# Giving one of the last attention block's two normalisation multiplies to ScalarE instead of VectorE

## The chip, the cores and the metric

The kernel runs on one core of one Trainium2 chip. The metric is device time in microseconds (us). The kernel before takes 1286.9 us (median of 6 runs, 1286.76 to 1287.05). Engines are named as the profile names them: PE is the matmul side of TensorE and PEld its weight loads, DVE is VectorE, ACT is ScalarE, POOL is GpSimd, SP is the engine that starts the DMAs.

I use one measure, which I call **the tail**: from the start of the first reciprocal of the last attention block to the end of the last add on VectorE.

## The reference, cut to what matters

```python
xn = layernorm(A_x)                              # 2048 x 512
q  = (xn @ wq) -> 32 heads of 128
p  = softmax(q @ k_cache^T * 128**-0.5)          # 2048 keys per head
o  = p @ v_cache
s  = concat_heads(o) @ wo                        # 2048 x 512
g  = silu(reglu_mlp(xn))                         # gate, up, down; 2048 x 512
return x + s * g
```

## The kernel before

The MLP runs first and leaves `g_sb`. Then 128 blocks follow, one for each head and each 512 queries (`QB` = 4 blocks a head). A block runs 16 score tiles, the exponential on ScalarE, and 16 PV steps which accumulate in two PSUM banks, two groups of 128 queries in each. Column 128 of V holds a constant, so each group's column 128 of the accumulator is the softmax denominator (`z_ap`). The last block is normalised bank by bank, to let the second half of the work start early:

```python
def emit_norm_last(b, bank, pvtok):
    ...
    _wait(dve, pvtok)                            # PV of this bank is complete
    o_ap, z_ap = acc_view()
    js = slice(2 * bank, 2 * bank + 2)
    rtok = sem_rz.sig(dve.reciprocal(rz_sb[:, js, :], z_ap[:, js, :]))
    _wait(dve, rtok)
    tok = sem_norm.sig(
        dve.tensor_tensor(Onorm[ob][:, js, :], o_ap[:, js, :],
                          rz_sb[:, js, :].to_broadcast([128, 2, Dh]), ALU.mult))
    emit_last_transposes(hh, Q, ob, bank, tok)   # queued; PE does them later
    return tok
```

After the last block, eight of the 16 output tiles remain (tiles 8 to 15, 128 rows each). Tiles 8 to 11 don't need the last block; tiles 12 to 15 do, through four transposes on PE and two copies on ScalarE:

```python
for n in range(NT - 8, NT - 4, 2):               # tiles 8,9 then 10,11
    emit_M([(emit_final_tile, n), (emit_final_tile, n + 1)])
    if n == NT - 8:
        flush_last_transposes()                  # PE: between tile 9 and tile 10
for n in range(NT - 4, NT, 2):                   # tiles 12..15
    emit_M([(emit_final_tile, n), (emit_final_tile, n + 1)])
flush_final_add()
```

A final tile is four matmuls on PE, a multiply with `g_sb` on VectorE (from PSUM into `fin_tmp`), and an add to `x_sb` on VectorE. The add of a tile is issued after the multiply of the next one:

```python
def emit_final_tile(n, bank):
    ...                                          # 4 matmuls into ps_r, signal otok
    _wait(dve, otok)
    _wait(dve, fin_free[fb])
    mtok = sem_opa.sig(
        dve.tensor_tensor(fin_tmp[fb][:], ps_r[:, bank, 0:D], g_sb[:, n, :], ALU.mult))
    flush_final_add()                            # x_sb += fin_tmp of the tile before, then its output DMA
    fin_pending.append((n, fb, mtok))
    return mtok
```

The softmax here doesn't subtract the row's maximum and nothing guards it: scores larger than these inputs give would overflow.

## Time and profile before

| what | value | how to read it |
|---|---|---|
| time | 1286.9 us | median of 6 runs |
| span of the profile | 1284.6 us | first to last instruction |
| PE busy | 1278.8 us, 100% | the whole is bound by TensorE |
| VectorE busy in the tail | 8.89 of 8.96 us | busy time by stretch; the tail runs at VectorE's pace |
| last multiply's end to the span's end | 2.8 us | the last add and the last output DMA |

The first lines of the page of the kernel before, and its chain of work that ended last, by engine (the chain is followed back from the last instruction, at each step to what released it; shares are of the span):

```profile
span 1284.6 us, 26946 instructions
...
PE 1278.8 (100%) x12040; PEld 835.2 (65%) x12040; DVE 380.6 (30%) x685; ACT 1001.7 (78%) x1109; POOL 13.2 (1%) x25
...
PE 99%; DVE 1%; ACT 0%; issue 0%; DVEq 0%
```

Over the whole span PE is the limit. The 1% of VectorE in the chain is the tail, which is the only place that the change touches. The next lines are from the timeline of the kernel before. The columns are start, duration (both in us), engine, line, operation, output and inputs, shapes, count of merged instructions, and in square brackets the idle time of the engine before it and what ended that. L779 is the matmuls of a final tile, L787 its multiply, L803 its add, L714 the transposes, L693 and L696 the reciprocal and the multiply of the normalisation.

```profile
1269.85 1.89 PE L779 MATMUL ps_r<-Wo_sb,OT_store 128*128 128x512 bf16 x8
1270.91 0.69 DVE L787 TENSOR_TENSOR fin_tmp<-ps_r,g_sb 128x512 bf16<-128x512 f32 x1 [3.31 <-PE ps_r L779]
...
1273.39 1.89 PE L779 MATMUL ps_r<-Wo_sb,OT_store 128*128 128x512 bf16 x8
1273.48 0.17 DVE L693 RECIPROCAL rz_sb<-ps_acc 128x2 f32<-128x2 f32 x1 [0.61 <-PE ps_acc L742]
1273.68 0.42 DVE L696 TENSOR_TENSOR Onorm<-ps_acc,rz_sb 128x256 bf16<-128x256 f32 x1
1274.02 0.16 DVE L693 RECIPROCAL rz_sb<-ps_acc 128x2 f32<-128x2 f32 x1
1274.22 0.42 DVE L696 TENSOR_TENSOR Onorm<-ps_acc,rz_sb 128x256 bf16<-128x256 f32 x1
1274.56 0.68 DVE L787 TENSOR_TENSOR fin_tmp<-ps_r,g_sb 128x512 bf16<-128x512 f32 x1
1274.90 0.42 PEld L714 LDWEIGHTS ps_r<-ident,Onorm 128*128 128x128 bf16 x4
1275.12 0.39 PE L714 MATMUL ps_r<-ident,Onorm 128*128 128x128 bf16 x4
...
1275.34 5.34 PE L779 MATMUL ps_r<-Wo_sb,OT_store 128*128 128x512 bf16 x24
...
1275.49 0.69 DVE L787 TENSOR_TENSOR fin_tmp<-ps_r,g_sb 128x512 bf16<-128x512 f32 x1
...
1276.42 0.69 DVE L787 TENSOR_TENSOR fin_tmp<-ps_r,g_sb 128x512 bf16<-128x512 f32 x1
...
1281.09 0.69 DVE L787 TENSOR_TENSOR fin_tmp<-ps_r,g_sb 128x512 bf16<-128x512 f32 x1
1281.69 0.75 DVE L803 TENSOR_TENSOR x_sb<-x_sb,fin_tmp 128x512 bf16<-128x512 bf16 x2
```

Three readings matter.

- The tail is 8.96 us: from 1273.48 to 1281.69 + 0.75 = 1282.44. Multiplies start every 0.933 us (1274.56 to 1281.09 is seven steps), with an add between two of them and no idle time noted on VectorE. PE delivers a tile every 0.864 us (four matmuls of 0.216 us each: eight take 1.73 us in the chain of work), so VectorE is the slower of the two in the tail, by little.
- Where VectorE did wait for a final tile, its multiply came 1.06 us after the tile's first matmul (1269.85 to 1270.91). Call this the lead.
- PE's first matmul of tile 8 is at 1273.39 and that of tile 10 at 1275.34. With the lead, their multiplies cannot start before 1274.45 and 1276.40. They start at 1274.56 and 1276.42. So PE is only 0.11 and 0.02 us ahead of VectorE there.

### The profile page before, as it was taken

Reading aid. Unit: us, or ns where it says so; the run is one execution under the profiler, and the core shown is the slowest. Engines: PE = TensorE matmul, PEld = TensorE weight load, DVE = VectorE, ACT = ScalarE, POOL = GpSimd, SP = SyncE. Lnnn points to the kernel's source line nnn. Section 1 sums busy time; section 2 is a strip of 40 time slices with the busy share of each in tenths; the row PEclk is TensorE's granted clock in tenths of the full one; section 3 lists DMA queues with packets and bytes.
Section 4 is the critical chain, followed back from the end, with each engine's and each line's share of the span. In section 5 each row is a group of like instructions: output and inputs, shape, how many; then the busy total and the mean of one; then the engine's idle time right before and its main releaser. Section 6 shows DMA issues by size and latency. Waiting matters only on the chain.

```text
span 1284.6 us, 26946 instructions
## 1 busy us (share of the span) xinstructions
PE 1278.8 (100%) x12040; PEld 835.2 (65%) x12040; DVE 380.6 (30%) x685; ACT 1001.7 (78%) x1109; POOL 13.2 (1%) x25
## 2 busy tenths in 40 slices
PE   9999999999999999999999999999999999999998
PEld 5444476666666666666666666666666666666665
DVE  6433311112222222222222222222222222234455
ACT  3322399998888888888888888888888888888884
POOL 2100000000000000000000000000000000000000
PEclk9999999999999999999999999999999999999999
DMA  9600123232222332332321322323323312333202
GB/s 262 131 1 1 22 48 53 62 55 38 36 53 46 71 55 50 55 70 51 54 47 31 66 47 53 55 67 55 55 51 71 54 34 38 51 67 55 51 13 75
DMA packets 240977, 72.13 MB, mean 56 GB/s; under 512 B 227808, under 2 KB 240864, under 8 KB 240864
## 3 DMA queue, kind: packets, MB, share of 16 engines
q1 hardware_dynamic: 240048, 69.76, 28.5%
q8 instruction: 96, 1.57, 0.5%
q10 hardware_dynamic: 816, 0.66, 0.2%
q14 instruction: 17, 0.14, 0.0%
HBM read 32.77 MB, written 2.10 MB: 27 GB/s over the span
## 4 chain that ended last, share of the span: by engine, by line
PE 99%; DVE 1%; ACT 0%; issue 0%; DVEq 0%
PE ps_acc L742 36%; PE ps_r L645 34%; PE ps_r L578 9%; PE ps_r L599 8%; PE ps_acc L511 4%; PE ps_r L488 4%; PE ps_r L492 4%; PE ps_r L779 1%; DVE fin_tmp L787 0%; PE ps_r L402 0%; PE ps_r L374 0%; DVE x_sb L803 0%; ACT gr_sb L454 0%; PE ps_acc L364 0%; ACT xcT L369 0%
## 5 line engine op out<-in xcount | busy, mean ns | idle before, releaser
L655 ACT ACTIVATE PT<-ps_r 128x1024 bf16<-128x1024 f32 x1024 | 952.5, 1054 | 167.7 <-PE ps_r L645 167.7
L742 PEld LDWEIGHTS ps_acc<-V_sb,PT 128*128 128x128 bf16 x8192 | 620.9, 98 | 241.8 <-ACT PT L655 3.5
L742 PE MATMUL ps_acc<-V_sb,PT 128*128 128x129 bf16 x8192 | 776.9, 220 | 0.0
L645 PE MATMUL ps_r<-QT_sb,KT_sb 128*128 128x512 bf16 x2048 | 754.5, 379 | 0.0
L672 DVE RECIPROCAL rz_sb<-ps_acc 128x4 f32<-128x4 f32 x127 | 23.2, 183 | 729.8 <-PE ps_acc L742 729.8
L645 PEld LDWEIGHTS ps_r<-QT_sb,KT_sb 128*128 128x128 bf16 x2048 | 194.9, 98 | 1.1 <-DVE QT_sb L589 0.4
L578 PE MATMUL ps_r<-xnT,Wq_sb 128*128 128x512 bf16 x512 | 130.9, 379 | 0.0
L599 PE MATMUL ps_r<-Wo_sb,OT_store 128*128 128x512 bf16 x448 | 114.6, 379 | 0.0
L589 DVE CAST QT_sb<-ps_r 128x512 bf16<-128x512 f32 x128 | 88.5, 691 | 48.2 <-PE ps_r L578 48.2
L578 PEld LDWEIGHTS ps_r<-xnT,Wq_sb 128*128 128x128 bf16 x512 | 49.8, 97 | 60.7 <-ACT PT L655 27.1
L675 DVE TENSOR_TENSOR Onorm<-ps_acc,rz_sb 128x512 bf16<-128x512 f32 x127 | 87.8, 691 | 4.4
L599 PEld LDWEIGHTS ps_r<-Wo_sb,OT_store 128*128 128x128 bf16 x448 | 43.8, 98 | 52.9 <-ACT PT L655 0.2
L454 ACT ACTIVATE gr_sb<-ps_r 128x512 bf16<-128x512 f32 x56 | 32.9, 595 | 49.2 <-PE ps_r L488 48.7
L612 DVE TENSOR_TENSOR s_acc<-s_acc,ps_r 128x512 f32<-128x512 f32 x96 | 66.0, 687 | 17.4 <-PE ps_r L599 17.4
L460 DVE TENSOR_TENSOR hT<-gr_sb,ps_r 128x512 bf16<-128x512 bf16 x56 | 38.4, 685 | 46.9 <-PE ps_r L492 42.2
L511 PE MATMUL ps_acc<-Wd_sb,hT 128*128 128x512 bf16 x224 | 49.0, 379 | 0.0
L492 PE MATMUL ps_r<-xnT,Wu_sb 128*128 128x512 bf16 x168 | 43.1, 379 | 0.0
L488 PE MATMUL ps_r<-xnT,Wg_sb 128*128 128x512 bf16 x168 | 43.1, 379 | 0.0
L511 PEld LDWEIGHTS ps_acc<-Wd_sb,hT 128*128 128x128 bf16 x224 | 21.9, 98 | 26.5 <-DVE g_sb L528 0.3
L519 ACT ACTIVATE sig_sb<-ps_acc 128x512 f32<-128x512 f32 x12 | 7.2, 597 | 29.5 <-PE ps_acc L511 29.5
L492 PEld LDWEIGHTS ps_r<-xnT,Wu_sb 128*128 128x128 bf16 x168 | 16.4, 98 | 19.8
L488 PEld LDWEIGHTS ps_r<-xnT,Wg_sb 128*128 128x128 bf16 x168 | 16.4, 98 | 19.8
(50 smaller groups left out, 182.1 us busy)
## 6 DMA issues: line engine op xcount, KB each, us to landing
V_sb<-in_A_v_cache_dram SPq DMA_DIRECT2D x32, 512.0 KB, 4.6
Wq_sb<-in_A_wq_dram SPq DMA_DIRECT2D x32, 128.0 KB, 2.5
Wo_sb<-in_A_wo_dram SPq DMA_DIRECT2D x8, 512.0 KB, 4.9
OT_store<-Onorm SPq DMA_TRANSPOSE x127, 2.4
Wd_sb<-in_B_W_down_dram SPq DMA_DIRECT2D x1, 1792.0 KB, 14.6
x_sb<-in_A_x_dram SPq DMA_DIRECT2D x3, 512.0 KB, 12.1
out_dram<-x_sb SPq DMA_DIRECT2D x6, 256.0 KB, 2.2
Wg_sb<-in_B_W_gate_dram SPq DMA_DIRECT2D x1, 768.0 KB, 12.0
```

What stands on the lines that cost most here:

```text
L460: dve.tensor_tensor(hT[par][:, fc, :], gr_sb[gk][:], ps_r[:, gb + 1, :], ALU.mult)
L488: ins = pe.matmul(ps_r[:, gb, :], Wg_sb[:, c, fs], xT[:, c, xs], start=(c == 0), stop=(c == DC - 1))
L492: ins = pe.matmul(ps_r[:, gb + 1, :], Wu_sb[:, c, fs], xT[:, c, xs], start=(c == 0), stop=(c == DC - 1))
L511: ins = pe.matmul(ps_acc[:, jb, 0:D], hT[par][:, fc, j * 128:(j + 1) * 128], Wd_sb[:, fc, :], start=(fc == 0), stop=(fc == FC - 1))
L578: ins = pe.matmul(ps_r[:, bank, :], Wq_sb[b][:, c, :], xnT[:, c, qs], start=(c == 0), stop=(c == DC - 1))
L589: etok = sem_qpe.sig(dve.tensor_copy(QT_sb[b][:, qs], ps_r[:, bank, :]))
L599: ins = pe.matmul(ps_r[:, bank, 0:D], OT_store[g % 2][:, hh, n * 128:(n + 1) * 128], Wo_sb[g % 2][:, hh, :], start=(hh == 0), stop=(hh == ...
L612: dve.tensor_tensor(s_acc[:, n, :], s_acc[:, n, :], ps_r[:, bank, 0:D], ALU.add)
L645: ins = pe.matmul(ps_r[:, 2 * s + tt, :], KT_sb[h % 2][:, t * 128:(t + 1) * 128], QT_sb[h % 2][:, qs], start=True, stop=True)
L655: act.activation(PT[pb][:], ps_r[:, 2 * s:2 * s + 2, :], ACTF.Exp, scale=scale)
L675: dve.tensor_tensor(Onorm[ob][:], o_ap, rz_sb[:].to_broadcast([128, 4, Dh]), ALU.mult))
L742: ins = pe.matmul(o_ap, PT[pb][:, tt, j * 128:(j + 1) * 128], V_sb[vb][:, t, 0:VW], start=(t == 0 and j % 2 == 0), stop=(t == KT - 1 and j ...
```

## The change

The intent: VectorE is busy all through the tail and ScalarE is idle from the last exponential until it copies the transposes. So ScalarE takes the multiply of bank 0, as two activations with function Copy and the reciprocal as a per-row scale. VectorE is to go straight on to bank 1.

```diff
                     rtok = sem_rz.sig(dve.reciprocal(rz_sb[:, js, :], z_ap[:, js, :]))
+                    if bank == 0:
+                        _wait(act, rtok)
+                        for j in range(2):
+                            tok = sem_otc.sig(
+                                act.activation(Onorm[ob][:, j, :], o_ap[:, j, :], ACTF.Copy,
+                                               scale=rz_sb[:, j, 0:1]))
+                        emit_last_transposes(hh, Q, ob, bank, tok)
+                        return tok
                     _wait(dve, rtok)
```

## The prediction

> **What bounds it now.** TensorE. The page's busy shares give PE 1278.8 of 1284.6 us (100%), ACT 78%, DVE 30%; the chain that ended last is 99% PE, 1% DVE. The change touches only the last block's tail, after its last PV matmul (about 1273.5 us), so at most the last 11 us can move. There the chain in order of time leaves PE and runs on VectorE: reciprocal 1273.48, multiply 1273.68, reciprocal 1274.02, multiply 1274.22, then eight final multiply/add pairs (fin_tmp, x_sb) at 1274.56, 1275.49, 1276.42, ..., 1281.09, every 0.933 us, then the last output DMA.
>
> **Removed.** One 128x256 multiply on VectorE, 0.42 us (start to next start 0.34 us in the timeline).
>
> **Added.** Two 128x128 ACTIVATE Copy on ScalarE, idle from 1271.4 to 1275.4 us. The Trainium skill, "ScalarE: Activation LUTs", section "What ACT_TABLE_LOAD costs", gives 186 ns + 0.833 ns per column, 93 ns more per pointer operand, 93 ns overlap: estimate 386 ns each, about 0.68 us for both. The trace agrees on the operand: Tanh 128x512 took 687 ns with a pointer scale, 597 without. No table load: the section "Table sets" says copy is in every set, and the built program shows none. They should run at about 1273.75 to 1274.45.
>
> **Moved.** The second reciprocal follows the first at once (about 1273.65, once the last PV matmul has signalled), its multiply at about 1273.85, done at 1274.27. PE's order is unchanged.
>
> **How much is on the critical path.** VectorE could start final tile 8 at about 1274.2, but must wait for PE. Where VectorE was idle before, the first multiply came 1.06 to 1.07 us after its tile's first matmul (1269.85 to 1270.91; 1264.58 to 1265.65). Tile 8's first matmul starts at 1273.39 and does not move, so its multiply can't start before 1274.45: 0.11 us earlier than now, not 0.34. Tile 9 could follow at 1275.38. Tile 10's matmuls begin at 1275.34, behind the four transposes, which stand behind tile 9's matmuls, not behind the normalisation (first weight load 1274.90; Onorm done at 1274.64). So tile 10's multiply can't start before 1276.40; today it starts at 1276.42. The remaining gain is about 0.02 us, and from there VectorE's 0.933 us cadence is what it was. The transposes need ScalarE's result by 1274.90; estimated ready at 1274.45, so PE should not wait.
>
> **Predicted time:** 1287.0 us (gain 0.0 to 0.1 us, below the 0.3 us spread of the runs); 8 in 10 between 1286.0 and 1288.0. Chances: faster by over 2% 0.005, within 2% 0.985, slower 0.01.
>
> **What would show each step.**
> - Timeline: two Onorm activations on ScalarE of 0.3 to 0.4 us each, both done before 1274.9; no table load.
> - VectorE's two reciprocals adjacent, one 0.42 us multiply, then a new short wait of VectorE for PE before tile 8's multiply, about 0.2 us.
> - Tile 8's multiply 1.06 us after its first matmul; tile 10's at 1276.40 on the old clock; from the last PV matmul to the end of the span unchanged within 0.1 us.
> - Transposes still directly behind tile 9's matmuls, no idle of PE ahead of them.
>
> **What would make it wrong.** A hidden table load (1.28 us each in this trace): ScalarE would end near 1275.7, the transposes and PE would slip about 0.6 us and the tail with them, still only 0.05%. ScalarE and VectorE slowing each other on the accumulator banks. A much later wake-up of ScalarE. None reaches 2%; the total can leave the range only by a state of the chip, not by this edit.

## The result, and the profile after

The changed kernel took 1286.92 us (median of 6 runs, 1286.44 to 1287.22), the kernel before 1286.9 us (6 runs of the same rounds). The ratio is 1.0, with a 95% interval of 0.9987 to 1.0013: the same.

The top of the page of the changed kernel:

```profile
span 1285.3 us, 26720 instructions
...
PE 1267.7 (99%) x11813; PEld 835.9 (65%) x12040; DVE 380.5 (30%) x684; ACT 1002.3 (78%) x1111; POOL 13.3 (1%) x25
```

The counts show the edit: one instruction fewer on VectorE (685 to 684) and two more on ScalarE (1109 to 1111). PE's lower busy time is not a gain. Its matmul records are 11813 against 12040 weight loads, so 227 records are missing from this trace, and the weight loads are complete. (The chain of this page also runs through ScalarE for 12% of the span where the other ran through PE alone; the exponentials are unchanged, so I draw nothing from it.)

The timeline of the changed kernel in the tail. The added lines moved the line numbers: here L787 is the matmuls of a final tile, L795 its multiply, L811 its add, L722 the transposes, L698 the new activations, L704 the one multiply left to VectorE.

```profile
1274.20 0.28 DVE L693 RECIPROCAL rz_sb<-ps_acc 128x2 f32<-128x2 f32 x2 [0.61 <-PE ps_acc L750]
1274.32 1.67 PE L787 MATMUL ps_r<-Wo_sb,OT_store 128*128 128x512 bf16 x7
1274.40 0.63 ACT L698 ACTIVATE Onorm<-ps_acc,rz_sb 128x128 bf16<-128x128 f32 x2 [2.29 <-DVE rz_sb L693]
1274.51 0.42 DVE L704 TENSOR_TENSOR Onorm<-ps_acc,rz_sb 128x256 bf16<-128x256 f32 x1
1275.17 0.69 DVE L795 TENSOR_TENSOR fin_tmp<-ps_r,g_sb 128x512 bf16<-128x512 f32 x1 [0.23 <-PE ps_r L787]
1275.62 0.42 PEld L722 LDWEIGHTS ps_r<-ident,Onorm 128*128 128x128 bf16 x4
...
1275.84 0.39 PE L722 MATMUL ps_r<-ident,Onorm 128*128 128x128 bf16 x4
...
1276.06 5.34 PE L787 MATMUL ps_r<-Wo_sb,OT_store 128*128 128x512 bf16 x24
1276.11 0.68 DVE L795 TENSOR_TENSOR fin_tmp<-ps_r,g_sb 128x512 bf16<-128x512 f32 x1
...
1277.12 0.69 DVE L795 TENSOR_TENSOR fin_tmp<-ps_r,g_sb 128x512 bf16<-128x512 f32 x1
...
1281.80 0.69 DVE L795 TENSOR_TENSOR fin_tmp<-ps_r,g_sb 128x512 bf16<-128x512 f32 x1
1282.40 0.75 DVE L811 TENSOR_TENSOR x_sb<-x_sb,fin_tmp 128x512 bf16<-128x512 bf16 x2
```

Of the eight matmuls of tiles 8 and 9 the first is not in this trace (x7, from 1274.32), so the lead of tile 8 can't be read here. That of tile 10 can: 1276.06 to 1277.12, again 1.06 us.

The tail began 0.72 us later in this execution (1274.20 against 1273.48), which is all of the difference between the two spans and not the change's doing (see kernel 2), so compare each event by its distance from the first reciprocal:

| us after the first reciprocal | before | after |
|---|---|---|
| last multiply of the normalisation on VectorE ends | 1.16 | 0.73 |
| ScalarE's two activations end | – | 0.83 |
| multiply of tile 8 starts | 1.08 | 0.97 |
| the transposes start on PE | 1.64 | 1.64 |
| multiply of tile 9 starts | 2.01 | 1.91 |
| multiply of tile 10 starts | 2.94 | 2.92 |
| multiply of tile 15 starts | 7.61 | 7.60 |
| last add on VectorE ends (the tail) | 8.96 | 8.95 |

VectorE's normalisation ends 0.43 us earlier. That is more than the 0.34 us of the multiply, because the second reciprocal now starts 0.11 us after the first (0.28 - 0.17), where a multiply used to start only 0.20 us after it. Of the 0.43 us, tile 8 gets 0.11 us. A new wait for PE takes 0.24 us (0.97 - 0.73; the profile puts 0.23 in brackets), and the last 0.08 us is an overlap that is lost: before, tile 8's multiply started 0.08 us ahead of the end of the normalisation (1.08 against 1.16). Tile 10 gets 0.02 us, because its matmuls stand behind the transposes, which have not moved. From there on VectorE is at its own pace again and the end moves by 0.01 us.

### The profile page after: what moved, and what is told of

It reads as the page before. It is cut to its first block, busy times and chain, and to the rows that moved or that the text cites. A ratio compares the mean times of both kernels' runs of the same rounds, so it can differ in the third digit from the quotient of the medians.

```text
span 1285.3 us, 26720 instructions
## 1 busy us (share of the span) xinstructions
PE 1267.7 (99%) x11813; PEld 835.9 (65%) x12040; DVE 380.5 (30%) x684; ACT 1002.3 (78%) x1111; POOL 13.3 (1%) x25
## 4 chain that ended last, share of the span: by engine, by line
PE 86%; ACT 12%; issue 1%; DVE 0%; DVEq 0%
PE ps_acc L750 32%; PE ps_r L645 25%; ACT PT L655 12%; PE ps_r L578 9%; PE ps_r L599 8%; PE ps_acc L511 4%; PE ps_r L492 4%; PE ps_r L488 4%; PE ps_r L787 1%; PE ps_r L374 0%; PE ps_r L402 0%; DVE fin_tmp L795 0%; DVE x_sb L811 0%; ACT gr_sb L454 0%; PE ps_acc L364 0%
## 5 line engine op out<-in xcount | busy, mean ns | idle before, releaser
L645 PE MATMUL ps_r<-QT_sb,KT_sb 128*128 128x512 bf16 x1837 | 675.1, 379 | 0.3
```

The source lines that it names most:

```text
L645: ins = pe.matmul(ps_r[:, 2 * s + tt, :], KT_sb[h % 2][:, t * 128:(t + 1) * 128], QT_sb[h % 2][:, qs], start=True, stop=True)
```

## The experiments

**Theory.** VectorE is the slower engine in the tail, but PE follows it so closely that time taken off VectorE ahead of tile 8 is turned into waits for PE, at tile 8 and at tile 10. **Rival.** The 0.34 us that a multiply costs in VectorE's stream is really there to be had, and ScalarE's version eats it: through its two activations, its wake-up, or both engines reading the accumulator. In the experiments "mult" and "add" are VectorE's instructions for a final tile. All nine kernels passed the comparison with the reference. That includes the first one, which leaves out a multiply, so that comparison is too coarse to see it.

### 1. Nobody does bank 0's multiply

```diff
 # against the changed kernel
                     if bank == 0:
-                        _wait(act, rtok)
-                        for j in range(2): ... act.activation(...)
-                        emit_last_transposes(hh, Q, ob, bank, tok)
-                        return tok
+                        emit_last_transposes(hh, Q, ob, bank, rtok)
+                        return rtok
```

> Bank 0's multiply left out altogether (no engine does it; wrong result in 256 rows on purpose). Tail = from the start of the first reciprocal of the last block to the end of the last add on VectorE; before 8.96 us, after 8.95 us. Theory (TensorE sets the pace at tiles 8 and 10, so VectorE time saved ahead of them is not worth anything): tail 8.93 to 8.97, tile 8's multiply 0.97 us after the first reciprocal, tile 10's 2.92 us. Rival (the saved 0.34 us is eaten by ScalarE's version: its two activations, its wake-up, the shared accumulator bank): tail near 8.6.

From the timeline of this kernel: the reciprocals, tile 8's multiply and the last adds.

```profile
1274.01 0.28 DVE L693 RECIPROCAL rz_sb<-ps_acc 128x2 f32<-128x2 f32 x2 [0.61 <-PE ps_acc L745]
...
1274.99 0.69 DVE L790 TENSOR_TENSOR fin_tmp<-ps_r,g_sb 128x512 bf16<-128x512 f32 x1 [0.24 <-PE ps_r L782]
...
1282.21 0.75 DVE L806 TENSOR_TENSOR x_sb<-x_sb,fin_tmp 128x512 bf16<-128x512 bf16 x2
```

The tail was 8.95 us, tile 8's multiply came 0.98 us and tile 10's 2.93 us after the first reciprocal, and VectorE waited 0.24 us for PE at tile 8. One run took 1286.94 us against 1286.84 us for the kernel before. So the multiply for free is worth as much as the multiply on ScalarE: nothing. The rival falls; ScalarE's version costs nothing that a cheaper one would have given back.

### 2. VectorE does bank 0's multiply twice

```diff
 # against the kernel before
                     _wait(dve, rtok)
+                    if bank == 0:
+                        sem_norm.sig(dve.tensor_tensor(scr[:, 0:2, :], o_ap[:, js, :],
+                                     rz_sb[:, js, :].to_broadcast([128, 2, Dh]), ALU.mult))
                     tok = sem_norm.sig(
```

> The kernel before, with VectorE doing bank 0's multiply a second time, into a scratch buffer. Theory (before, VectorE runs back to back through the tail, with TensorE 0.02 to 0.1 us ahead, so the tail is open to added VectorE time though not to saved time): every multiply from tile 8 on is 0.34 us later, tail 9.28 to 9.32. Rival (VectorE has real slack in the tail and the whole of it is TensorE's): tail under 9.05.

From the timeline of this kernel: first reciprocal, tile 8's multiply, and the last adds.

```profile
1274.96 0.17 DVE L694 RECIPROCAL rz_sb<-ps_acc 128x2 f32<-128x2 f32 x1 [0.61 <-PE ps_acc L747]
...
1276.38 0.68 DVE L792 TENSOR_TENSOR fin_tmp<-ps_r,g_sb 128x512 bf16<-128x512 f32 x1
...
1283.51 0.75 DVE L808 TENSOR_TENSOR x_sb<-x_sb,fin_tmp 128x512 bf16<-128x512 bf16 x2
```

Tile 8's multiply is 1.42 us after the reciprocal (1.08 before) and the tail is 9.30 us (8.96 before): the added 0.34 us comes through whole. One multiply more costs 0.34 us, one multiply fewer gives 0.01 us. VectorE's work is on the path, and still there is nothing to gain by shortening it ahead of tile 8. The single run took 1288.23 us, 1.39 us more than the kernel before; only 0.34 us of that is the tail. The tail simply began late in this execution (1274.96). The profiled executions of all kernels here begin it between 1273.43 and 1274.96 us. The traces show where that comes from: the first score matmul starts between 144.0 and 145.5 us, and from there to the first reciprocal of the last block all eleven profiled executions take 1129.4 or 1129.5 us. So the shift arises in the first 144 us, in code that the change doesn't touch. In this execution the first matmul on the gate weights waited 1.37 us for their DMA and started at 7.71 us, against 6.21 us in the kernel before.

### 3 and 4. The transposes between tiles 10 and 11, without and with the change

```diff
 # the same edit, once against the kernel before and once against the changed kernel
-                for n in range(NT - 8, NT - 4, 2):
-                    emit_M([(emit_final_tile, n), (emit_final_tile, n + 1)])
-                    if n == NT - 8:
-                        flush_last_transposes()
+                emit_M([(emit_final_tile, NT - 8), (emit_final_tile, NT - 7)])
+                s = ring_acquire()
+                m0 = emit_final_tile(NT - 6, 2 * s)
+                flush_last_transposes()
+                m1 = emit_final_tile(NT - 5, 2 * s + 1)
+                ring_tok[s] = [m0, m1]
```

> The kernel before, with the four transposes of the last block moved from between final tiles 9 and 10 to between 10 and 11. Theory: VectorE is back to back here, so an earlier tile 10 is of no use: tail 8.95 to 8.97. Rival (before is TensorE-bound at tile 10 as well): tail shorter by up to 0.2, 8.75 to 8.85.

> The changed kernel with the same move of the transposes. Theory: tile 10's matmuls start 0.22 us earlier, so its multiply no longer waits for TensorE and comes at 2.83 us after the first reciprocal; tile 11 becomes the gate at about 3.79 (3.87 before): tail 8.86 to 8.89, so 0.07 to 0.1 of the saved time comes through. Rival (nothing of the saved time is there to be had, or ScalarE's share eats it): tail 8.95.

Without the change the tail was 8.97 us, from the first and the last line here: no gain.

```profile
1273.97 0.17 DVE L693 RECIPROCAL rz_sb<-ps_acc 128x2 f32<-128x2 f32 x1 [0.61 <-PE ps_acc L742]
...
1282.19 0.75 DVE L803 TENSOR_TENSOR x_sb<-x_sb,fin_tmp 128x512 bf16<-128x512 bf16 x2
```

With it, from the timeline:

```profile
1273.87 0.28 DVE L693 RECIPROCAL rz_sb<-ps_acc 128x2 f32<-128x2 f32 x2 [0.61 <-PE ps_acc L750]
...
1276.37 0.39 PE L722 MATMUL ps_r<-ident,Onorm 128*128 128x128 bf16 x4
...
1276.71 0.68 DVE L795 TENSOR_TENSOR fin_tmp<-ps_r,g_sb 128x512 bf16<-128x512 f32 x1
...
1277.65 0.69 DVE L795 TENSOR_TENSOR fin_tmp<-ps_r,g_sb 128x512 bf16<-128x512 f32 x1
...
1282.00 0.75 DVE L811 TENSOR_TENSOR x_sb<-x_sb,fin_tmp 128x512 bf16<-128x512 bf16 x2
```

Tile 10's multiply now comes at 2.84 us, tile 11's at 3.78 us, and the tail is 8.88 us. So 0.07 us of the saved time comes through once tile 10's matmuls no longer stand behind the transposes. This shows that the queue order of PE was what held the last part of the gain. Even without it less than 0.1 us is left, since tile 8's multiply, still held by its own matmuls, comes only 0.11 us earlier than in the kernel before. The single runs took 1286.92 us without and 1286.72 us with the change, the kernel before 1286.84 us on the same chip; no total resolves 0.07 us.

### 5. Six more activations on ScalarE

```diff
 # against the changed kernel
                         _wait(act, rtok)
+                        for k in range(6):
+                            sem_otc.sig(act.activation(scr[:, k, :], o_ap[:, k % 2, :], ACTF.Copy,
+                                                       scale=rz_sb[:, k % 2, 0:1]))
                         for j in range(2):
```

> The changed kernel with six more activations of the same shape on ScalarE (into a scratch buffer) ahead of its two. Theory: ScalarE's result has about 0.5 us of slack before the transposes; six more at 0.27 us each end 2.45 us after the first reciprocal where the transposes need it at 1.42, so TensorE idles about 1.05 us ahead of the transposes, tile 10's multiply comes at about 3.97 us, and the tail is 9.9 to 10.1. Rival (the hand-over through the transposes isn't on the path that ends last): tail stays 8.95.

From the timeline of this kernel:

```profile
1273.58 0.28 DVE L694 RECIPROCAL rz_sb<-ps_acc 128x2 f32<-128x2 f32 x2 [0.61 <-PE ps_acc L755]
...
1275.30 0.66 ACT L703 ACTIVATE Onorm<-ps_acc,rz_sb 128x128 bf16<-128x128 f32 x2
...
1276.10 0.38 PE L727 MATMUL ps_r<-ident,Onorm 128*128 128x128 bf16 x4 [0.72 <-ACT Onorm L703]
...
1277.39 0.69 DVE L800 TENSOR_TENSOR fin_tmp<-ps_r,g_sb 128x512 bf16<-128x512 f32 x1 [0.88 <-PE ps_r L792]
...
1282.66 0.75 DVE L816 TENSOR_TENSOR x_sb<-x_sb,fin_tmp 128x512 bf16<-128x512 bf16 x2
```

PE now idles 0.72 us for ScalarE ahead of the transposes, tile 10's multiply waits 0.88 us for PE, and the tail is 9.83 us, 0.88 us more. The direction was as expected, the size missed the range of 9.9 to 10.1. I had taken the start of the transposes' first weight load (1.42 us after the reciprocal) as the moment when ScalarE's result is needed. That load runs ahead, behind the matmuls of tile 9; the first transpose itself starts at 1.64 us in the changed kernel and at 2.52 us here, which is the 0.88 us. Here it started 0.14 us after ScalarE's end (2.38 us). So my estimate, from this one trace, is that ScalarE's result was needed by about 1.64 - 0.14 = 1.50 us. In the changed kernel it was there at 0.83 us: some 0.67 us of slack, not 0.5. The single run took 1287.5 us, the kernel before 1286.88 us (median of 8). The path through ScalarE is real, and has slack enough to be harmless in the change.

### 6 and 7. Three adds on GpSimd, without and with the change

If VectorE's pace is what sets the tail, taking work off it *after* tile 10 should help where taking it off before tile 8 did not.

```diff
 # the same edit, once against the kernel before and once against the changed kernel
+                    on_pool = n in (NT - 6, NT - 4, NT - 2)          # tiles 10, 12, 14
+                    eng, sem = (pool, sem_padd) if on_pool else (dve, sem_opa)
-                    _wait(dve, mtok)
-                    ftok = sem_opa.sig(
-                        dve.tensor_tensor(x_sb[:, n, :], x_sb[:, n, :], fin_tmp[fb][:], ALU.add))
+                    _wait(eng, mtok)
+                    ftok = sem.sig(
+                        eng.tensor_tensor(x_sb[:, n, :], x_sb[:, n, :], fin_tmp[fb][:], ALU.add))
+                    add_tok[n] = ftok                # the output DMA waits for both adds it sends
```

> The kernel before, with the final adds of tiles 10, 12 and 14 moved from VectorE to the idle GpSimd. Theory: VectorE's 0.933 us per tile falls below TensorE's 0.864 us, so the tail waits for TensorE: the last multiply 7.25 to 7.35 us after the first reciprocal in place of 7.61, the last add ends at 8.3 to 8.45 in place of 8.96; time 0.5 to 0.65 us shorter than before, a ratio near 0.9996, too small for a verdict other than same. Rival (GpSimd's adds slow VectorE through SBUF or come late): tail 8.9 or more.

> The changed kernel with the same three adds on GpSimd. Theory: with TensorE setting the pace in the tail, ScalarE's help is worth nothing at all: tail within 0.03 us of the same edit on the kernel before. Rival (the change frees VectorE time that becomes useful once VectorE is less loaded): tail 0.1 us or more shorter than that.

From the timeline of the sixth kernel: first reciprocal, GpSimd's add of tile 14, tile 15's multiply and the last add.

```profile
1273.68 0.17 DVE L694 RECIPROCAL rz_sb<-ps_acc 128x2 f32<-128x2 f32 x1 [0.61 <-PE ps_acc L743]
...
1280.83 1.26 POOL L807 TENSOR_TENSOR x_sb<-x_sb,fin_tmp 128x512 bf16<-128x512 bf16 x1 [0.46 <-DVE fin_tmp L788]
1281.00 0.68 DVE L788 TENSOR_TENSOR fin_tmp<-ps_r,g_sb 128x512 bf16<-128x512 f32 x1
1281.71 0.66 DVE L807 TENSOR_TENSOR x_sb<-x_sb,fin_tmp 128x512 bf16<-128x512 bf16 x1
```

The last multiply comes at 7.32 us in place of 7.61, as expected, and the tail is 8.69 us in place of 8.96. I had expected 8.3 to 8.45, and the rival 8.9 or more, so neither was right. The difference is in the last line: VectorE's last add took 0.66 us in place of 0.42, beside GpSimd's add, and it started 0.71 us after its multiply in place of 0.60, since it now needs the result of the instruction just before it. With the change the tail is 8.70 us (1274.01 to 1282.71). So the two agree within 0.01 us, and the change is worth nothing here either.

The whole times don't show the 0.27 us: 1286.43 us without the change (ratio 0.9997, 95% interval 0.9983 to 1.0011) and 1286.9 us with it (ratio 1.0, 0.9987 to 1.0013), against 1286.88 us for the kernel before in the same rounds.

### 8 and 9. Another placing of the adds, without and with everything else

```diff
 # against kernel 6; kernel 9 has in addition the change and the moved transposes of kernel 4
-                    on_pool = n in (NT - 6, NT - 4, NT - 2)
+                    on_pool = n in (NT - 5, NT - 3)                  # tiles 11, 13
 ...
+                    if n == NT - 1:
+                        flush_final_add()            # tile 14's add ahead of tile 15's multiply
                     _wait(dve, otok)
```

> The kernel before with the adds of tiles 11 and 13 on GpSimd (1.26 us each there in the earlier run, so both are over before the last add) and tile 14's add on VectorE ahead of tile 15's multiply. Theory: tiles 13 and 14 wait for TensorE, the last multiply starts 7.40 us after the first reciprocal and the last add ends at 8.35 to 8.50, against 8.96 for the kernel before, 0.5 us or 0.04% of the whole. Rival (a GpSimd add slows any VectorE work beside it): tail 8.7 or more. The whole time is not expected to show it: verdict same, median 1286.0 to 1286.9.

> The same edit on the changed kernel, with the transposes also moved between tiles 10 and 11, so that the time saved on VectorE has the freest way through. Theory: TensorE is the gate at tiles 13 and 14 in both, so the tail is within 0.04 us of the same edit on the kernel before (8.35 to 8.50). Rival (the change saves time once TensorE's gate is moved and VectorE relieved): 0.07 us or more shorter than that.

From the timeline of the eighth kernel:

```profile
1274.22 0.17 DVE L694 RECIPROCAL rz_sb<-ps_acc 128x2 f32<-128x2 f32 x1 [0.61 <-PE ps_acc L743]
...
1280.50 1.26 POOL L809 TENSOR_TENSOR x_sb<-x_sb,fin_tmp 128x512 bf16<-128x512 bf16 x1 [0.38 <-DVE fin_tmp L790]
1280.67 0.68 DVE L790 TENSOR_TENSOR fin_tmp<-ps_r,g_sb 128x512 bf16<-128x512 f32 x1
1281.39 0.66 DVE L809 TENSOR_TENSOR x_sb<-x_sb,fin_tmp 128x512 bf16<-128x512 bf16 x1
1281.97 0.68 DVE L790 TENSOR_TENSOR fin_tmp<-ps_r,g_sb 128x512 bf16<-128x512 f32 x1
1282.68 0.42 DVE L809 TENSOR_TENSOR x_sb<-x_sb,fin_tmp 128x512 bf16<-128x512 bf16 x1
```

This was a miss. The tail was 8.88 us, not 8.35 to 8.50, and the rival of that expectation held. Tile 14's add, which should have taken 0.33 us of VectorE's stream, started 0.72 us after its own multiply (it waits for it) and took 0.66 us beside GpSimd's add. The last multiply so came at 7.75 us, and the last add started another 0.71 us later. That last add, with no GpSimd add beside it, took 0.42 us: the late start goes with its dependence, the length of 0.66 us with GpSimd's add. The part that matters for the change held: the ninth kernel, with everything, had a tail of 8.90 us (1273.43 to 1282.33), within 0.02 us of the eighth. Medians were 1286.73 us (ratio 1.0001, 0.9987 to 1.0014) and 1286.63 us (0.9998, 0.9986 to 1.0011), against 1286.95 us for the kernel before: the same. No version here beats either kernel by a measured total. The shortest tail is that of kernel 6, on the kernel before, by 0.27 us or 0.02%.

## Why the prediction was right

- **The bound.** "TensorE", with VectorE setting the tail, was right. Kernel 2 showed that VectorE's work is on the path of the tail (+0.34 us comes through whole).
- **"0.11 us earlier than now, not 0.34"** at tile 8: 0.11 us. The predicted short wait of VectorE for PE ahead of tile 8, "about 0.2 us", was 0.23 us.
- **"Tile 10's multiply can't start before 1276.40"**: on the clock of the kernel before (subtract 0.72) it started at 1276.40. Kernel 4 showed that the transposes' place in PE's order was the cause: moving them let 0.07 us through.
- **"The remaining gain is about 0.02 us"**: 0.01 us by the tails. Predicted 1287.0 us, measured 1286.92 us, and the difference of the medians (0.02 us the other way) is far within the spread. The total is no test of the mechanism: any cause that leaves the time as it was would have fallen in 1286.0 to 1288.0. The events in the timeline are the test. Among them, from the first reciprocal to the end of the span it is 11.12 us before and 11.10 us after, as predicted unchanged within 0.1 us.
- **ScalarE's part.** "About 0.68 us for both" was 0.63 us, "1273.75 to 1274.45" was 1273.68 to 1274.31 on the old clock, and no table load came: both traces have the same two loads, neither of them in the tail. The trace agrees here with the Trainium skill's "ScalarE: Activation LUTs", which puts copy in every table set (section "Table sets: the hidden batching unit").
- **What was mis-sized.** The time taken off VectorE ahead of tile 8 was 0.43 us and not 0.34, but all above 0.11 us went into the wait and the lost overlap. That ScalarE's result was needed "by 1274.90", the first weight load, was too strict. The estimate from kernel 5 is 1274.98 (1.50 us after the reciprocal). Neither mattered for the time.
- **What stays open.** The small moves are read from one profile each. The same event repeats to 0.01 or 0.02 us between kernels that share it (tile 8's multiply at 0.97 to 0.98 us in kernels 1 and 4 and in the changed one), but no total time here resolves less than about 0.1%.

## What to carry to other kernels

When one engine looks busy without a gap, its slack is not what decides the gain of relieving it: ask how far ahead its supplier is at each hand-over. Here PE was 0.11 us ahead at one hand-over and 0.02 us at the next, and a saving of 0.43 us on VectorE shrank to the smaller of the two. A quick test is to add the work a second time and to leave it out: if adding costs its full price and leaving it out gives nothing, another engine stands level at that place. It says nothing of other places: kernel 6 took work off VectorE further on, where its pace lags PE's, and the tail became 0.27 us shorter. And before costing a change, see how much of the span its stage has: here 9 of 1285 us.

## What the Trainium skill lacked or had wrong

- "ScalarE: Activation LUTs", section "What ACT_TABLE_LOAD costs": its formula (186 ns + 0.833 ns per column + 93 ns per pointer operand) gives 386 ns for a 128x128 activation with a pointer scale. The runs show 359 and 368 ns reading from PSUM. Its overlap of 93 ns gives 293 ns from start to start; six in a row took 1.66 us, which is about 0.26 us from start to start ((1.66 - 0.36) / 5). The page does not say for which memory its figures are.
- "SBUF — State Buffer", section "Who interferes with whom": it says that a VectorE instruction with two SBUF inputs contends with a GpSimd one that reads SBUF, for ports that are an exclusive lock. The runs agree in direction (VectorE's add took 0.66 us in place of 0.42 in kernels 6 to 9, and each time ended 0.28 or 0.29 us after GpSimd's add ended), but the page does not say how this looks in a trace: as a longer bar of the blocked instruction, not as idle time ahead of it.
- "GPSIMD Engine Reference", section "Elementwise — side-by-side cycle accounting": it has about 2.6 cycles per element for a two-input add, and 1.96 times VectorE's time for 2048 fp32 columns. For 128x512 bf16 the runs show 1.26 us against 0.42 us on VectorE, 3 times. A VectorE add ran across its start in every case, so part of the 1.26 us may be a wait; no run here has a GpSimd add by itself.
- "VectorE: DVE Perf Modes", section "The DRAIN you can't avoid": it says that a semaphore after each instruction costs nothing extra. It has no figure for an instruction that waits for the one just before it: the add started 0.71 or 0.72 us after its own multiply, against 0.60 us after another tile's.
- No page that I read has the time from a tile's first matmul to the start of the VectorE instruction that waits for the tile: 1.06 us for four 128x512 matmuls here.
